# Ninety-five of 1024 softmax exponential tiles computed on VectorE instead of ScalarE, in a fused attention block on one core

## The chip, the cores and the metric

The kernel runs on one core of a Trainium2 chip. The metric is device time in microseconds for one execution of the whole program. A core has a matrix engine (TensorE, "PE" in the profile), a vector engine (VectorE, "DVE"), an activation engine (ScalarE, "ACT"), a general engine (GpSimd, "POOL") and a queue engine for transfers (SyncE, "SP"). Each works through its own instructions in order and waits on semaphores that the others raise. TensorE writes its results to PSUM, eight banks of 128 partitions by 512 fp32 values here; VectorE and ScalarE read them from there and write to SBUF.

## The reference

One block of multi-head self-attention in bf16, for a sequence of 2048, a width of 448 and 16 heads of 28:

```python
B, S, D = x.shape                 # 1, 2048, 448
H = 16
Dh = D // H                       # 28
qkv = (x @ wqkv).reshape(B, S, 3, H, Dh).transpose(2, 0, 3, 1, 4)
q, k, v = qkv[0], qkv[1], qkv[2]
scores = einsum("bhqd,bhkd->bhqk", q, k) * (Dh ** -0.5)
p = softmax(scores, axis=-1)
o = einsum("bhqk,bhkd->bhqd", p, v)
return o.transpose(0, 2, 1, 3).reshape(B, S, D) @ wo
```

## The kernel before

**Tiling.** The 16 heads form 4 groups of 4, and the 2048 queries form 4 chunks of 512. One group and one chunk make a unit; there are 16 units, group by group. In a unit the keys run over 16 blocks of 128. A tile is one head, one key block and one query chunk: 128 keys by 512 queries of scores. So a unit has 64 tiles, and the kernel 1024. The tiles are ordered by unit, then key block, then head.

**A tile's way.** TensorE forms the scores of a tile with one matmul (L579) over the 28 rows of the head's part of K and Q; the four heads of a group lie 32 partitions apart, so the matmuls of neighbouring tiles use different rows of the array. ScalarE takes the exponential of a group of tiles at once (L584: two tiles a group in unit 0, three after that), with the factor Dh^-0.5 as the activation's scale, and writes bf16 into one of 36 slots of `PT`. When the four tiles of a key block are done, four matmuls (L546, "PV") multiply them with V and add into the accumulator bank 7, one head in each quarter of the partitions. V carries a column of ones beside its 28, so the accumulator's row 28 of each head is the softmax denominator. No maximum is subtracted.

**A unit's end** (`post_unit`). VectorE copies the accumulator to SBUF (L501). TensorE gathers the denominators (L509), VectorE takes the reciprocals (L514), TensorE spreads them (L524), VectorE multiplies (L529). In the last four units, where all groups of a query chunk are complete, four output projections follow (L479), each evicted (L488, L490) and stored.

**Projections.** x is transposed on TensorE (L368) and projected to Q, K and V (L385, L402), and each result is evicted from PSUM (L354 on ScalarE for a few, L356 on VectorE for the rest). What unit 0 and 1 need is done early; 38 "late jobs" (14 Q, 12 K and 12 V pieces) have due times spread over the units.

**Banks.** Score groups alternate between banks 0 to 2 and 3 to 5 (0 to 1 and 2 to 3 in unit 0). Bank 7 is the accumulator. Bank 6, the pool "M", is the only one for late projections, both matmul steps of a unit's end, and the output projection. Early jobs use banks 4 to 6.

**What sets the order.** Every operation is added to a small planner (`_Prog`) with its engine, the operations it depends on, an assumed duration, and a priority that is a position in units: for a score group, its tile's position less 0.2. `schedule` walks through time with these assumed durations, and on each engine takes, among the operations that can start within 150 ns of the earliest, the one with the lowest priority number. An operation with `acq` takes a bank from a pool, and a `rel` gives it back. Assumed latencies are 120 ns between engines and 200 ns between dependent operations on one engine. The order that comes out is fixed in each engine's queue; on the chip only the semaphores act. Score groups are chained among themselves, exponentials among themselves, and PVs among themselves.

Of the kernel before, what the change touches and what calls it, by code (L numbers as in the profile page):

```python
# [6 lines left out]
AF = mybir.ActivationFunctionType  # L7
ALU = mybir.AluOpType
AX = mybir.AxisListType
FP32 = mybir.dt.float32  # L10
BF16 = mybir.dt.bfloat16
I32 = mybir.dt.int32

ENGINES = ("pe", "act", "dve", "pool", "sp")

# [213 lines left out]
RHI = 2.0 ** 40  # L229


def _fast(nc, x, wqkv, wo, out, n_heads=16):

    B, S, D = x.shape
    assert B == 1
    H = n_heads
    DH = D // H
    G = H // 4
# [7 lines left out]
    HC = H * 32  # L246
    GD = 4 * DH
    NPT = 36
    NOB = 4
    scale = float(DH) ** -0.5  # L250
    VONE = DH
    assert DH * H == D and G * 4 == H and DH + 1 <= 32 and NIT * IT == D and GD <= IT

    xf = x.rearrange("b s d -> (b s) d")
# [7 lines left out]
    with es:  # L262
        def sb(name, shape, dt):
            return es.enter_context(nc.sbuf_tensor(name, shape, dt))
# [6 lines left out]
        KT = sb("KT", [128, G, S], BF16)  # L271
        V = sb("V", [128, NK, HC], BF16)
        PT = sb("PT", [128, NPT * 512], BF16)
        OTS = sb("OTS", [128, 2, 512], FP32)
        RS = sb("RS", [128, NU * 16], FP32)
        OTN = sb("OTN", [128, G, S], BF16)
# [12 lines left out]
        def bank(b, n=1):  # L289
            return ps[:, b * 512:(b + n) * 512]  # L290
# [4 lines left out]
        def i32v(ap):  # L295
            return ap.bitcast(I32)

# [24 lines left out]
        ms_v0 = P.add("pool", lambda e: e.memset(V4[:, :, DH:32], 0.0), dur=1500, prio=-9, name="ms_v0")  # L322
        ms_v1 = P.add("pool", lambda e: e.memset(V4[:, :, VONE:VONE + 1], 1.0), deps=[ms_v0], dur=800, prio=-9, name="ms_v1")
        ms_wop = P.add("pool", lambda e: e.memset(i32v(wop.rearrange("p g d -> p (g d)")), 0), dur=900, prio=-8, name="ms_wop")
        ms_one = P.add("pool", lambda e: e.memset(ONE[:, :], 1.0), dur=100, prio=-7, name="ms_one")
        sel_op = P.add("dve", (lambda e: e.tensor_copy(SEL[:, :], id_f.rearrange("p (h r) -> p h r", r=32)[:, :, VONE])),
                       deps=[id_f_op], dur=100, prio=-6, name="sel")
# [11 lines left out]
        P.pool("M", [6])  # L339
        early_ev = []  # L340

        def job(name, prio, mm_ops, evac, early, evac_eng="dve", evac_dur=660, after=()):

            hold = []
            prev = None
            for k, (f, deps, dur) in enumerate(mm_ops):
                op = P.add("pe", (lambda e, f=f: f(e, hold[0].banks[0])),
                           deps=list(deps) + (list(early_ev) if (k == 0 and not early) else []), after=[prev] + list(after),
                           dur=dur, prio=prio, name=f"{name}_{k}", acq=(("E" if early else "M", 1) if k == 0 else None))
                if k == 0:  # L350
                    hold.append(op)
                prev = op
            if evac_eng == "act":
                fe = (lambda e: e.activation(evac[0](), evac[1](hold[0].banks[0]), AF.Identity))  # L354
            else:
                fe = (lambda e: e.tensor_copy(evac[0](), evac[1](hold[0].banks[0])))  # L356
            ev = P.add(evac_eng, fe, deps=[prev] + list(evac[2:]), dur=evac_dur, prio=prio, name=f"{name}_ev", rel=[(hold[0], 0)])
            if early:
                early_ev.append(ev)
            return ev  # L360
# [16 lines left out]
        def proj_qk(t, g, c, prio, early, eng="dve"):  # L377
            dst = KT if t == 1 else QT
            mms = []
            for it in range(NIT):  # L380
                def f(e, b, it=it):
                    ins = None
                    for h in range(4):
                        col = t * D + g * GD + h * DH
                        ins = e.matmul(ps[32 * h:32 * h + 32, b * 512:(b + 1) * 512], w_raw[0:IT, it, col:col + 32],  # L385
                                       xT[0:IT, it, c * 512:(c + 1) * 512], start=(it == 0), stop=(it == NIT - 1), tile_position=(0, 32 * h))
                    return ins
                mms.append((f, [xt_ev[(it, c)]] + ([dma_w[t]] if it == 0 else []), 300))
            kq_ev[(t, g, c)] = job(f"p{t}_{g}_{c}", prio, mms,
                                   ((lambda: dst[:, g, c * 512:(c + 1) * 512]), (lambda b: bank(b))), early, evac_eng=eng)  # L390

        v_ev = {}

# [28 lines left out]
        def late_jobs():  # L422
            todo = []
            for u, (g, c) in enumerate(units):
                if u < 2:
                    continue
                todo.append((u - 0.6, "q", g, c))
            for g in range(1, G):
                for c in range(NCH):
                    todo.append((g * NCH - 2.9 + 0.5 * c, "k", g, c))  # L430
                    todo.append((g * NCH - 2.7 + 0.5 * c, "v", g, c))
            for pr, kind, g, c in sorted(todo):
                if kind == "v":
                    proj_v(g, c, pr, False)
                else:
                    proj_qk(1 if kind == "k" else 0, g, c, pr, False)
        late_jobs()


        tiles = [(u, kt, h) for u in range(NU) for kt in range(NK) for h in range(4)]  # L440
        NT = len(tiles)
        groups = []
        n = 0
        k = 0
        while n < NT:
            if tiles[n][0] < LATE0:
                b0, w = (0, 2)[k % 2], 2
            else:
                b0, w = (0, 3)[k % 2], 3
            k += 1  # L450
            w = min(w, NT - n)
            groups.append((n, w, b0))
            n += w

        bank_last = {}
        pt_last = [None] * NPT
        pt_pos = 0
        tile_slot = {}
        tile_ev = {}
# [77 lines left out]
        def pv(u, kt):  # L537
            g, c = units[u]
            slots = [tile_slot[(u, kt, h)] for h in range(4)]

            def f_pv(e):
                ins = None
                for h in range(4):
                    hh = 4 * g + h
                    pi = slots[h]
                    ins = e.matmul(ps[32 * h:32 * h + 32, ACC * 512:(ACC + 1) * 512], V[:, kt, hh * 32:(hh + 1) * 32],  # L546
                                   PT[:, pi * 512:(pi + 1) * 512], start=(kt == 0), stop=(kt == NK - 1), tile_position=(0, 32 * h))
                return ins
            op = P.add("pe", f_pv, deps=list({id(tile_ev[(u, kt, h)]): tile_ev[(u, kt, h)] for h in range(4)}.values())
                       + [v_ev[(g, kt // 4)]] + ([acc_ev[0]] if kt == 0 else []),  # L550
                       after=[last_pv[0]], dur=300, prio=u + (kt + 3) / NK, name=f"PV{u}_{kt}")
            last_pv[0] = op
            for s in slots:
                pt_last[s] = op
            if kt == NK - 1:
                post_unit(u, op)

        last_pv = [None]
        pv_next = 0
        for gi, (n0, w, b0) in enumerate(groups):  # L560
            tl = tiles[n0:n0 + w]
            if pt_pos + w > NPT:
                pt_pos = 0
            p0 = pt_pos
            pt_pos += w
            deps = [bank_last.get(b0 + j) for j in range(w)]
            for (u, kt, h) in tl:
                g, c = units[u]
                deps += [kq_ev[(0, g, c)], kq_ev[(1, g, kt // 4)]]
            if tl[-1][0] >= LATE0:  # L570
                deps += early_ev
            u0, kt0, h0 = tl[0]
            pr = u0 + (kt0 + h0 / 4) / NK - 0.2

            def f_s(e, tl=tl, b0=b0):
                ins = None
                for j, (u, kt, h) in enumerate(tl):
                    g, c = units[u]
                    ins = e.matmul(bank(b0 + j), KT[32 * h:32 * h + DH, g, kt * 128:(kt + 1) * 128],  # L579
                                   QT[32 * h:32 * h + DH, g, c * QCH:(c + 1) * QCH], start=True, stop=True, tile_position=(32 * h, 0))  # L580
                return ins
            s = P.add("pe", f_s, deps=deps, after=[last_s[0]], dur=260, prio=pr, name=f"S{gi}")
            last_s[0] = s
            ex = P.add("act", (lambda e, p0=p0, w=w, b0=b0: e.activation(PT[:, p0 * 512:(p0 + w) * 512], bank(b0, w), AF.Exp, scale=scale)),  # L584
                       deps=[s] + [pt_last[p0 + j] for j in range(w)], after=[last_exp[0]], dur=100 + w * 427, prio=pr, name=f"E{gi}")
            last_exp[0] = ex
            for j, t in enumerate(tl):
                tile_slot[t] = p0 + j
                tile_ev[t] = ex
                bank_last[b0 + j] = ex  # L590
            while 4 * pv_next + 3 < n0 + w:
                u, kt, _ = tiles[4 * pv_next]
                pv(u, kt)
                pv_next += 1
# [734 lines left out]
```

## Time and profile before

| what | value |
|---|---|
| runs | 523.44, 524.41, 541.12 us, median 524.41 |
| profiled execution | 523.52 us, its span 521.7 us |
| mean granted TensorE clock | 0.685 of full |
| ScalarE busy | 467.2 us, of which the exponentials 463.1 us in 352 instructions |
| TensorE matmul busy | 420.0 us; scores 182.0, PV 135.3 |
| VectorE busy | 74.7 us in 130 instructions |
| ScalarE waiting for score matmuls | 25.2 us, 31 times |

The page gives busy time, which for instructions that overlap is less than the sum of their durations. A chain of waits follows the work back from the last instruction; a group's mean duration is that of one instruction, with the idle time of its engine just before it and what ended that.

### The profile page before, as it was taken

The numbers are of one execution on the slowest core, as the hardware profiler recorded it, in microseconds if no ns is written. First come the engines' busy times: TensorE is split into PE (matmuls) and PEld (weight loads), VectorE is DVE, ScalarE is ACT, GpSimd is POOL, SyncE is SP. The second block draws the span as 40 slices with busy tenths as digits, with TensorE's granted clock in tenths as the row PEclk, the third lists the DMA queues.
The fourth block names the chain that finished last, engine by engine and source line by source line (L and its number), as shares of the span: only waits on it lengthen the run. The fifth ranks groups of instructions, "written<-read, shape, count | busy, mean of one in ns | idle before, by whom it ended". The sixth has DMA issues, their size and how long they took to land.

```text
span 521.7 us, 7778 instructions
## 1 busy us (share of the span) xinstructions
PE 420.0 (80%) x3585; PEld 141.7 (27%) x3585; DVE 74.7 (14%) x130; ACT 467.2 (90%) x358; POOL 3.4 (1%) x9
## 2 busy tenths in 40 slices
PE   5998888898978788797978879787887968879763
PEld 2433333333323132131312213131221413214131
DVE  2433222322221000010100001010000200202020
ACT  2999999999998999989899998989989799898930
POOL 2000000000000000000000000000000000000000
PEclk9999999999895555555565555556555675857655
DMA  8000000000000000000000000000000000100001
GB/s 264 2 3 2 1 1 1 2 1 1 3 0 1 1 0 1 0 2 0 1 1 0 1 0 1 0 1 0 1 1 0 13 25 1 36 0 27 10 1 40
DMA packets 6518, 5.84 MB, mean 11 GB/s; under 512 B 592, under 2 KB 6480, under 8 KB 6480
## 3 DMA queue, kind: packets, MB, share of 16 engines
q1 hardware_dynamic: 5552, 4.48, 2.8%
q10 hardware_dynamic: 928, 0.80, 0.5%
q8 instruction: 30, 0.49, 0.4%
q14 instruction: 8, 0.07, 0.0%
HBM read 3.44 MB, written 1.84 MB: 10 GB/s over the span
## 4 chain that ended last, share of the span: by engine, by line
ACT 76%; PE 20%; DMA 1%; DVE 1%; issue 1%; ACTq 0%
ACT PT L584 75%; PE ps L579 5%; PE ps L524 5%; PE ps L509 4%; PE ps L479 3%; PE ps L546 2%; DMA w_raw<-in_wqkv_dram 1%; PE ps L385 1%; DVE OUTS L490 1%; DVE OTN L529 0%; ACT OUTS L488 0%; PE ps L402 0%; DVE OTS L501 0%; DVE KT L356 0%; ACTq L312 0%
## 5 line engine op out<-in xcount | busy, mean ns | idle before, releaser
L584 ACT ACTIVATE PT<-ps 128x1536 bf16<-128x1536 f32 (+1 forms) x352 | 463.1, 1544 | 25.6 <-PE ps L579 25.2
L579 PE MATMUL ps<-QT,KT 28*128 28x512 bf16 x1024 | 182.0, 517 | 83.0 <-ACT PT L584 81.7
L546 PE MATMUL ps<-PT,V 128*32 128x512 bf16 x1024 | 135.3, 523 | 0.9 <-ACT PT L584 0.9
L579 PEld LDWEIGHTS ps<-QT,KT 28*128 28x128 bf16 x1024 | 35.8, 96 | 228.5 <-ACT PT L584 216.5
L546 PEld LDWEIGHTS ps<-PT,V 128*32 128x32 bf16 x1024 | 27.2, 98 | 85.5 <-issue 83.0
L501 DVE COPY OTS<-ps 128x512 f32<-128x512 f32 x16 | 11.1, 692 | 262.4 <-PE ps L546 262.4
L385 PE MATMUL ps<-xT,w_raw 112*32 112x512 bf16 x512 | 41.5, 401 | 0.7 <-DMA w_raw<-in_wqkv_dram 0.2
L524 PE MATMUL ps<-id_f,RS 128*32 128x128 f32 x512 | 27.8, 387 | 0.4 <-DVE RS L514 0.4
L509 PE MATMUL ps<-SEL,OTS 128*128 128x4 f32 x128 | 26.6, 331 | 1.1 <-DVE OTS L501 0.8
L509 PEld LDWEIGHTS ps<-SEL,OTS 128*128 128x128 f32 x128 | 25.2, 293 | 8.2 <-DVE OTS L501 6.9
L524 PEld LDWEIGHTS ps<-id_f,RS 128*32 128x32 f32 x512 | 20.0, 154 | 7.3 <-issue 3.5
L479 PE MATMUL ps<-wop,OTN 128*128 128x448 bf16 x64 | 18.6, 424 | 3.3 <-DVE OUTS L490 1.4
L402 PE MATMUL ps<-w_raw,xT 112*128 112x112 bf16 x256 | 17.8, 214 | 0.3 <-DVE OTN L529 0.2
L385 PEld LDWEIGHTS ps<-xT,w_raw 112*32 112x32 bf16 x512 | 12.6, 98 | 14.4 <-issue 6.3
L529 DVE TENSOR_TENSOR OTN<-ps,OTS 128x512 bf16<-128x512 f32 x16 | 11.1, 692 | 35.0 <-PE ps L524 35.0
L356 DVE CAST KT<-ps 128x512 bf16<-128x512 f32 x16 | 11.1, 692 | 33.7 <-PE ps L385 33.7
L402 PEld LDWEIGHTS ps<-w_raw,xT 112*128 112x128 bf16 x256 | 13.1, 98 | 7.0 <-issue 5.7
L488 ACT ACTIVATE OUTS<-ps 128x448 bf16<-128x448 f32 x2 | 1.1, 544 | 14.7 <-PE ps L479 14.7
L356 DVE CAST QT<-ps 128x512 bf16<-128x512 f32 x15 | 10.4, 692 | 25.6 <-PE ps L385 25.6
L356 DVE CAST V<-ps 128x448 bf16<-128x448 f32 x16 | 10.0, 625 | 27.8 <-PE ps L402 27.8
L490 DVE CAST OUTS<-ps 128x448 bf16<-128x448 f32 x14 | 8.8, 625 | 19.9 <-PE ps L479 19.9
L368 PE MATMUL ps<-id_b,x_nat 128*112 128x128 bf16 x64 | 6.1, 248 | 5.7 <-DMA x_nat<-in_x_dram 5.7
(25 smaller groups left out, 31.4 us busy)
## 6 DMA issues: line engine op xcount, KB each, us to landing
x_nat<-in_x_dram SPq DMA_DIRECT2D x4, 448.0 KB, 7.4
out_dram<-OUTS SPq DMA_DIRECT2D x16, 112.0 KB, 1.7
w_raw<-in_wqkv_dram ACTq DMA_DIRECT2D x2, 392.0 KB, 6.4
w_raw<-in_wqkv_dram SPq DMA_DIRECT2D x1, 392.0 KB, 8.9
wop<-in_wo_dram SPq DMA_DIRECT2D x16, 24.5 KB
```

The lines of the kernel that those rows point to most:

```text
L356: fe = (lambda e: e.tensor_copy(evac[0](), evac[1](hold[0].banks[0])))
L385: ins = e.matmul(ps[32 * h:32 * h + 32, b * 512:(b + 1) * 512], w_raw[0:IT, it, col:col + 32], xT[0:IT, it, c * 512:(c + 1) * 512], start= ...
L402: ins = e.matmul(ps[:, b * 512 + j * GD:b * 512 + (j + 1) * GD], xT[0:IT, it, n * 128:(n + 1) * 128], w_raw[0:IT, it, 2 * D + g * GD:2 * D ...
L479: ins = e.matmul(bank(b)[:, 0:D], OTN[:, gg, n * 128:(n + 1) * 128], wop[:, gg, :], start=(gg == 0), stop=(gg == G - 1))
L490: fe = (lambda e: e.tensor_copy(OUTS[:, oi, :], bank(hold[0].banks[0])[:, 0:D]))
L501: accev = P.add("dve", (lambda e: e.tensor_copy(OTS[:, ub, :], bank(ACC))), deps=[last_pv, ots_last[ub]], dur=660, prio=pr, name=f"ACCEV{u}")
L509: ins = e.matmul(bank(b)[:, qt * 4:(qt + 1) * 4], OTS[:, ub, qt * 128:(qt + 1) * 128], SEL[:, :], start=True, stop=True)
L524: ins = e.matmul(ps[32 * h:32 * h + 32, b * 512 + qt * 128:b * 512 + (qt + 1) * 128], RS[:, i:i + 1].to_broadcast([128, 32]), id_f[:, :], ...
L529: nm = P.add("dve", (lambda e: e.tensor_tensor(OTN[:, g, c * QCH:(c + 1) * QCH], bank(n2.banks[0]), OTS[:, ub, :], ALU.mult)), deps=[n2], ...
L546: ins = e.matmul(ps[32 * h:32 * h + 32, ACC * 512:(ACC + 1) * 512], V[:, kt, hh * 32:(hh + 1) * 32], PT[:, pi * 512:(pi + 1) * 512], start ...
L579: ins = e.matmul(bank(b0 + j), KT[32 * h:32 * h + DH, g, kt * 128:(kt + 1) * 128], QT[32 * h:32 * h + DH, g, c * QCH:(c + 1) * QCH], start ...
L584: ex = P.add("act", (lambda e, p0=p0, w=w, b0=b0: e.activation(PT[:, p0 * 512:(p0 + w) * 512], bank(b0, w), AF.Exp, scale=scale)), deps=[s ...
```

## The change

95 of the 1024 tiles no longer go to ScalarE. A walk over the tiles with assumed costs (3.1 us a tile for VectorE, 0.464 for ScalarE, and a load for what VectorE does besides) picks them: one in unit 0, and 5 to 7 in each later unit, mostly 8 tiles apart, none among the last 12. The rest are grouped in threes as before, across the tiles picked out.

For a picked tile TensorE forms the scores in bank 6, with 29 rows in place of 28. Q's eviction multiplies by 65536 log2(e) Dh^-0.5, so that a score comes out as a fixed-point exponent with 16 fractional bits; the 29th row holds constants whose product adds the exponent's bias. That row is put there by a new matmul of one contraction row at the head of each Q and K projection. ScalarE's exponential gets the inverse scale.

VectorE then runs five operations. D1 limits the score to 0 and 255 in that format and converts it to int32. D2 takes the low 16 bits as the fraction f and forms w = ES f + EC. D3 and D4 form (w + EA) w and then (w + EB) w, a quartic in f. D5 adds that to the fixed-point number divided by 512 and writes int16, whose bits are read as bf16 by PV. There are 3 buffers for D1 and D2 to D4 (`DT`, `DW`) and 8 result slots (`PD`). A picked tile has its own score operation (SD), which isn't chained to the score groups, and a priority 14 tiles earlier than its position. PV's priority is one key block later than it was.

```diff
@@ job
             if evac_eng == "act":
-                fe = (lambda e: e.activation(evac[0](), evac[1](hold[0].banks[0]), AF.Identity))
+                fe = (lambda e: e.activation(evac[0](), evac[1](hold[0].banks[0]), AF.Identity, scale=1.0 if mul is None else mul))
+            elif mul is not None:
+                fe = (lambda e: e.tensor_scalar(evac[0](), evac[1](hold[0].banks[0]), mul, None, ALU.mult))
@@ proj_qk
+                    if it == 0:
+                        e.matmul(bank(b), CW[:, t, :], ONR[:, :], start=True, stop=False)
                     for h in range(4):
                         col = t * D + g * GD + h * DH
-                        ins = e.matmul(ps[32 * h:32 * h + 32, b * 512:(b + 1) * 512], w_raw[0:IT, it, col:col + 32],
-                                       xT[0:IT, it, c * 512:(c + 1) * 512], start=(it == 0), stop=(it == NIT - 1), tile_position=(0, 32 * h))
+                        ins = e.matmul(ps[32 * h:32 * h + DH, b * 512:(b + 1) * 512], w_raw[0:IT, it, col:col + DH],
+                                       xT[0:IT, it, c * 512:(c + 1) * 512], start=False, stop=(it == NIT - 1), tile_position=(0, 32 * h))
@@ selection
+        dve_load = [1.7 + (4 * 0.62 if u // NCH == G - 1 else 0.0) for u in range(NU)]
+        dve_load[0] += 22.0
+        for u_ in late_units:
+            dve_load[u_] += 0.69
+        DCOST, ACOST, LEAD = 3.1, 0.464, 1.0
+        t_a = t_d = 0.0
+        on_dve = set()
+        for i, (u, kt, h) in enumerate(tiles):
+            if i % 64 == 0:
+                t_d = max(t_d, t_a) + dve_load[u]
+            if t_d + DCOST <= t_a + LEAD and i < NT - 12:
+                t_d = max(t_d, t_a - 2.0) + DCOST
+                on_dve.add(i)
+            else:
+                t_a += ACOST
@@ pv
-                                   PT[:, pi * 512:(pi + 1) * 512], start=(kt == 0), stop=(kt == NK - 1), tile_position=(0, 32 * h))
+                                   p_ap, start=(kt == 0), stop=(kt == NK - 1), tile_position=(0, 32 * h))
...
-                       after=[last_pv[0]], dur=300, prio=u + (kt + 3) / NK, name=f"PV{u}_{kt}")
+                       after=[last_pv[0]], dur=300, prio=u + (kt + 4) / NK, name=f"PV{u}_{kt}")
@@ picked tiles
+                pr -= 14 / 64.0
+                di, pi = nd % NDB, nd % NPD
+                nd += 1
+                s = P.add("pe", (lambda e, tl=tl, hold=hold: s_mm(e, tl, [hold[0].banks[0]], DH + 1)), deps=deps,
+                          dur=220, prio=pr, name=f"SD{gi}", acq=("M", 1), slack=200.0)
+                hold.append(s)
+                T, W = DT[:, di, :], DW[:, di, :]
+                F16 = DT[:, di, :].bitcast(U16).rearrange("p (n two) -> p n two", two=2)[:, :, 0]
+                o1 = P.add("dve", (lambda e, T=T, s=s: e.tensor_scalar(T, bank(s.banks[0]), 0.0, 255.0 * 65536.0 - 1.0, ALU.max, ALU.min)),
+                           deps=[s, d_last[di]], dur=620, prio=pr, name=f"D1_{gi}", rel=[(s, 0)])
+                o2 = P.add("dve", (lambda e, F16=F16, W=W: e.tensor_scalar(W, F16, ES, EC, ALU.mult, ALU.add)),
+                           deps=[o1, d_last[di]], dur=610, prio=pr, name=f"D2_{gi}")
+                o3 = P.add("dve", (lambda e, W=W: e.scalar_tensor_tensor(W, W, EA, W, ALU.add, ALU.mult)),
+                           deps=[o2], dur=610, prio=pr, name=f"D3_{gi}")
+                o4 = P.add("dve", (lambda e, W=W: e.scalar_tensor_tensor(W, W, EB, W, ALU.add, ALU.mult)),
+                           deps=[o3], dur=610, prio=pr, name=f"D4_{gi}")
+                o5 = P.add("dve", (lambda e, W=W, T=T, pi=pi: e.scalar_tensor_tensor(PD[:, pi, :], T, 1.0 / 512.0, W, ALU.mult, ALU.add)),
+                           deps=[o4, slot_last.get(("D", pi))], dur=610, prio=pr, name=f"D5_{gi}")
+                d_last[di] = o5
+                tile_slot[tl[0]] = ("D", pi)
+                tile_ev[tl[0]] = o5
```

## The prediction

> **What bounds the kernel now.** I read the page first, for the share of each engine and the course of the clock.
>
> ```profile
> span 521.7 us, 7778 instructions
> ...
> PE 420.0 (80%) x3585; PEld 141.7 (27%) x3585; DVE 74.7 (14%) x130; ACT 467.2 (90%) x358; POOL 3.4 (1%) x9
> ...
> DVE  2433222322221000010100001010000200202020
> ACT  2999999999998999989899998989989799898930
> PEclk9999999999895555555565555556555675857655
> ```
>
> ScalarE is full from the second slice to the last but one, VectorE nearly empty from slice 13 on, and TensorE's granted clock falls to half at about 160 us. So I cut the span into stages (the table of stretches; columns: length, busy time of PE, weight loads, VectorE, ScalarE and POOL, clock, DMA).
>
> ```profile
> 12.90:42.60 29.70, 28.49 (x324) 11.69 (x324) 10.24 (x21) 29.54 (x32) 0.00 (x0) 1.00 0.01 2
> 42.60:161.10 118.50, 99.66 (x1260) 39.59 (x1260) 31.22 (x50) 117.14 (x88) 0.00 (x0) 0.96 0.01 2
> 191.50:345.20 153.70, 125.17 (x841) 35.95 (x841) 8.14 (x16) 144.95 (x108) 0.00 (x0) 0.51 0.00 1
> 345.20:500.05 154.85, 124.95 (x876) 39.02 (x876) 15.63 (x27) 142.97 (x105) 0.00 (x0) 0.61 0.03 10
> ```
>
> At full clock ScalarE is idle 1.4 us in 118.5. At half clock it is idle 8.8 in 153.7 and 11.9 in 154.9. The chain that ended last tells where (columns: start, length, work).
>
> ```profile
> 43.05 88.77 ACT PT L584 x66
> ...
> 167.14 24.29 ACT PT L584 x18
> 191.43 0.05 issue
> 191.48 0.61 PE ps L579 x3
> 192.09 1.87 PE ps L509 x8
> 193.96 0.55 PE ps L546 x3
> 194.51 0.54 PE ps L579 x3
> 195.05 1.86 PE ps L524 x32
> ```
>
> An exponential of three tiles costs 88.77 / 66 = 1.345 us of the path, or 24.29 / 18 = 1.349 at half clock: 0.450 us a tile. (Its own 1.58 us overlaps its neighbours.) At each unit's end the two normalisation steps, 1.87 us each at half clock, hold TensorE, and ScalarE starves about 2 us: its waits for score matmuls sum to 22.3 us between 161 and 500. Everything else is behind the exponentials, so taking tiles off ScalarE can pay.
>
> The prices come from the groups with shapes kept apart, and from VectorE's timeline.
>
> ```profile
> L584 ACT ACTIVATE PT<-ps 128x1536 bf16<-128x1536 f32 x320 | 433.5, 1583 | 24.0 <-PE ps L579 23.7
> L356 DVE CAST KT<-ps 128x512 bf16<-128x512 f32 x16 | 11.1, 692 | 33.7 <-PE ps L385 33.7
> L529 DVE TENSOR_TENSOR OTN<-ps,OTS 128x512 bf16<-128x512 f32 x16 | 11.1, 692 | 35.0 <-PE ps L524 35.0
> ```
>
> ```profile
> 13.27 1.09 DVE L356 COPY xT<-ps 112x512 bf16<-112x512 bf16 x3 [0.61 <-PE ps L368]
> ...
> 503.71 0.29 DVE L597 TENSOR_SCALAR CK<-RS 128x256 f32<-128x256 f32 x1
> 504.04 0.43 DVE L598 SCALAR_TENSOR_TENSOR CK<-RS,CK 128x256 f32<-128x256 f32 x1
> ```
>
> **Removed.** 95 tiles leave ScalarE: one in unit 0 (groups of two, 29.66 us for 64 tiles, 0.46 each) and 94 later: 0.46 + 94 x 0.450 = 42.8 us off the path, if nothing else becomes late.
>
> **Added on VectorE: five operations a tile.** D1 reads 512 fp32 from PSUM: 0.692, by the cast's row. D3, D4 and D5 take two inputs: 256 elements took 0.426 and the TENSOR_TENSOR at 512 took 0.692, so 0.692 each. D2 has one input in SBUF: by the 256-element TENSOR_SCALAR (0.294; same fixed 0.16, half the slope) 0.43, or 0.692 if the stepped 16-bit source loses that rate. Bodies: 3.20 to 3.46 us. A dependent operation starts 0.04 after the one before (504.00 to 504.04), so a chain alone takes 3.40 to 3.66. Independent operations overlap (three copies of 0.42 in 1.09, 0.085 saved on each), so two interleaved chains may take 2.77 to 3.03 a tile. Ends 2.77 and 3.66; there are three work buffers, so chains will partly interleave, and I take the middle, 3.25. Total 309 us beside the 74.7 already there: 384 us in a kernel of over 480, so VectorE is not the bound on average.
>
> In stretches it nearly is. Running the diff's selection rule by hand gives 5 to 7 tiles a unit after the first, and 79 of the 94 spacings are 8 tiles, thus 7 on ScalarE: 7 x 0.450 = 3.15 us. Each dense spacing lacks 3.25 - 3.15 = 0.10 us: 79 x 0.10 = 8 us. The ends are 0 and 79 x 0.51 = 40 us.
>
> What is queued behind: the score matmul of the next such tile (SD) needs bank 6, which D1 frees; TensorE takes its queue in order, so an SD early in its queue holds PV and the next scores, and then ScalarE. Normalisation, late projections and output projection share that bank, and the unit's eviction stands in VectorE's queue among the D operations. Eight result slots let tiles be made far ahead of their PV, which covers single delays.
>
> **Added on TensorE.** An SD stands alone where three scores stand side by side: one packet of three took 0.32 us until the next start at full clock and 0.54 at half, and one alone costs no less than 512 columns of that. 95 x 0.32 to 0.54 is 30 to 51 us, less 31 packets saved (10 to 17). At half clock a unit needs (19.3 + 6.3) x 0.54 + 16 x 0.55 + 3.74 = 26.4 us of TensorE, against 24.1 now; ScalarE needs 58 x 0.45 = 26.1. It fits in about 28, with 1.6 us to spare. I cost it at nothing; if the spare goes, the first rival holds.
>
> **Added to the projections**: one matmul of one row ahead of each of 32 Q and K jobs, 0.3 us each. The two at the start lie on the path and four run in unit 0, where TensorE is 28.49 of 29.70 busy: 0 to 1.8 us, I take 1.5. The 26 later ones sit beside exponentials. Four small memsets run before the first x lands (5.7 us), under that load. The Q scaling replaces a copy of the same size: nothing.
>
> **The clock.** In the trace TensorE goes to half speed after 150 us although its longest wait for ScalarE there (the weight loads of L579) is 1.2 us, and is back at full speed for 4 us only after some 6 us without a gap (162 to 168). The Trainium skill, "TensorE: Matmul & The Clock Gate", section "Why this matters for your kernels", asks for idle gaps over about 3 us before the clock falls. This trace disagrees, with its 1.2 us; by the page the half clock and its unit-end waits would be absent and the sum about 470. The trace decides.
>
> A rule that speaks against the change stands in "VectorE: DVE Perf Modes", section "The DRAIN you can't avoid": the next operation cannot issue until the pipe is empty, so five operations always cost five whole ones. By it the sum would be near the first rival's end, 522; the three overlapping copies (1.09 us, not 1.26) say it is not so strict.
>
> **Sum.** The profiled execution took 523.5 us (span 521.7), close to the median of 524.4. 523.5 - 42.8 + 1.5 + 8 = 490.2, rounded to 490. The tail after the last exponential (500 us on) is untouched, since the last 12 tiles stay on ScalarE.
>
> **Rivals.**
> 1. VectorE paces, or TensorE at half clock does. For: dense spacings of 3.15 us against up to 3.66; 1.6 us of TensorE spare. Against: the gaps of 16 to 24 tiles and eight slots. With the full 40 us lost: 523.5 - 42.8 + 1.5 + 40 = 522; its middle 512.
> 2. Slower: an SD reaches the head of TensorE's queue while bank 6 waits behind two queued VectorE operations (2 x 0.69 = 1.38 us). A score packet now waits 0.36 us on average for ScalarE in the half-clock stage (63.6 us over 179 waits between 161 and 500), so that much lateness is covered. It loses from the point where each of 95 waits exceeds 0.45 + 0.36 = 0.81; at 1.38 the time is 523.5 + 95 x 0.57 = 578. For: one bank for all of it, and an order fixed beforehand from assumed durations (0.61 an operation) that are shorter than the rows. Against: VectorE is free a fifth of the time.
> 3. More TensorE work closes its gaps, the clock stays up, and the 22.3 us of unit-end waits mostly vanish (19.8 of them fall between 160 and 470): 490 - 19.8 = 470. For: 168 to 172 us. Against: 1.7 busy of 2 us did not lift it.
> 4. The change does not do what it says, because VectorE's PSUM reads slow the exponentials: at 10%, 929 x 0.045 = 42 us, no gain, 524. Against: 1.345 us a group with VectorE a quarter busy, 1.349 with it idle.
>
> **How the numbers follow.** Forecast 0.45 (own range 482 to 503); rival 1 0.17 (503 to 523); rival 2 0.19 (523 to 580); rival 3 0.14 (465 to 482); rival 4 0.05. The measurement can tell about 2%, so faster means under 514: 0.45 + 0.14 + 0.10 of rival 1 = 0.69. Within: 0.07 + 0.03 of rival 2 + 0.04 of rival 4 = 0.14. Slower than 535: 0.16 + 0.01 = 0.17. The range 476 to 535 leaves out some 0.06 of rival 3 below and 0.14 of rival 2 above.
>
> **What would show it.** Groups of three stay at 1.35 us and number about 289. VectorE's busy time is near 384 us; D2's row at 0.43 or 0.69 settles it. ScalarE's waits for score matmuls are near 35 us; over 60, traced to TensorE waiting for D1's line, is rival 2. A granted clock well over 0.685 is rival 3. The prediction is wrong if a tile takes over 3.6 us on VectorE, if SDs wait for bank 6 at length, or if unit ends hold ScalarE longer than 2 us.

## The result, and the profile after

The changed kernel takes 539.76 us (median of 4 runs, 537.47 to 541.39), the kernel before beside it 524.41 (523.44 to 527.49, and one run of 541.12). Some runs of one and the same kernel take some per cent longer than its others, so runs more than 1.5% above a kernel's fastest are given but not compared, here and below. The ratio is 1.0276, with a 95% interval of 1.0206 to 1.0345: slower, by some 15 us, where the forecast was 34 us faster. The profiled execution took 539.61 us, its span is 537.7.

The page of the changed kernel, by its first lines, the course of ScalarE and of the clock, and the chain that ended last by engine:

```profile
span 537.7 us, 8275 instructions
...
PE 478.3 (89%) x3617; PEld 156.7 (29%) x3617; DVE 346.0 (64%) x609; ACT 432.7 (80%) x327; POOL 3.4 (1%) x9
...
ACT  2897777777988888897898899778798979798940
PEclk9995555555555655795657597555656576595855
...
PE 54%; ACT 33%; DVE 10%; DMA 1%; issue 1%; ACTq 0%
```

ScalarE is no longer full, and the first half clock stands in the fourth slice, where before it stood in the thirteenth. TensorE now makes up 54% of the chain. The same stretches as in the prediction (length, busy time of PE, weight loads, VectorE, ScalarE, POOL, clock, DMA):

```profile
12.90:42.60 29.70, 28.02 (x302) 11.70 (x301) 15.11 (x30) 27.81 (x31) 0.00 (x0) 0.98 0.03 5
42.60:161.10 118.50, 111.64 (x784) 35.21 (x784) 77.84 (x136) 92.06 (x67) 0.00 (x0) 0.50 0.00 1
191.50:345.20 153.70, 138.95 (x1137) 46.68 (x1135) 111.99 (x193) 133.71 (x99) 0.00 (x0) 0.66 0.00 1
345.20:500.05 154.85, 141.32 (x1007) 44.00 (x1005) 110.74 (x195) 132.23 (x96) 0.00 (x0) 0.60 0.02 7
```

The second row carries the result. Before, the clock there was 0.96 and ScalarE worked 117.14 of 118.50 us; now the clock is 0.50 throughout, TensorE is busy 111.64 us and ScalarE works 92.06. That is 25 us of ScalarE's time lost in one stretch. The prices of VectorE's part are in the groups with shapes kept apart (busy, mean ns of one, idle time before, its releaser):

```profile
L649 ACT ACTIVATE PT<-ps 128x1536 bf16<-128x1536 f32 x288 | 398.5, 1481 | 72.9 <-PE ps L637 71.0
...
L665 DVE TENSOR_SCALAR DT<-ps 128x512 int32<-128x512 f32 x95 | 65.5, 689 | 34.0 <-PE ps L637 33.6
L671 DVE SCALAR_TENSOR_TENSOR DW<-DW 128x512 f32<-128x512 f32 x95 | 65.2, 686 | 0.8
L673 DVE SCALAR_TENSOR_TENSOR PD<-DT,DW 128x512 int16<-128x512 int32 x95 | 64.8, 682 | 0.1
L669 DVE SCALAR_TENSOR_TENSOR DW<-DW 128x512 f32<-128x512 f32 x95 | 64.5, 679 | 0.8
...
L667 DVE TENSOR_SCALAR DW<-DT 128x512 f32<-128x512 uint16 x95 | 40.2, 423 | 1.4
```

D1, D3, D4 and D5 cost 0.68 to 0.69 us, D2 0.42. The waits (in total, times, longest) tell who is late:

```profile
ACT PT L649 <- PE ps L637: 73.7, 85, 2.7
...
PEld ps L637 <- DVE DT L665: 20.1, 37, 1.3
...
PEld ps L413 <- DVE DT L665: 11.0, 18, 1.3
...
PE ps L637 <- DVE DT L665: 5.2, 14, 0.8
```

ScalarE waits 73.7 us for scores, against 25.2 before. So the account closes on ScalarE: its exponentials' busy time fell from 463.1 to 428.5 us (34.6 less), its waits for scores rose by 48.5, and the first exponential starts 1.4 us later (14.3 against 12.9). That is 15.3 us more, and the span grew by 16.0. The page's row for all exponentials:

```profile
L649 ACT ACTIVATE PT<-ps 128x1536 bf16<-128x1536 f32 (+1 forms) x321 | 428.5, 1440 | 75.6 <-PE ps L637 73.7
```

TensorE waits for D1 in small pieces on several lines: 41.1 us by its weight loads and 9.7 us by its matmuls, never over 1.3 us at a time. D1 (L665) holds 4% of the chain, some 21 us.

Two things in TensorE's records are new. First, the projections have moved. Each row below gives the matmuls' shortest, median and longest duration (ns) and their first and last start (us); first the kernel before, then the changed one.

```profile
L385 PE MATMUL ps<-xT,w_raw x512: 377/381/634, 7.6 to 150.9; 112*32 112x512 bf16 x171
```

```profile
L416 PE MATMUL ps<-xT,w_raw x512: 379/605/634, 8.3 to 471.6; 112*28 112x512 bf16 x171
```

They ended at 151 us, at full clock; now the last starts at 471.6 and the median duration is that of half clock. In the order of TensorE's queue the last projection stood behind score tile 307 before, and stands behind tile 932 now. The planner did that: a picked tile's score matmul (SD) has a priority 14 tiles ahead of its position, needs no other bank than 6, and so takes it from the late projections, whose numbers are higher. Second, the clock drops at 42 us; before, it dipped from 134.5 to 138 us and fell for longer at 155. All engines by single microseconds, first the kernel before, then the changed one (same columns):

```profile
39.00:40.00 1.00, 1.00 (x12) 0.25 (x12) 0.06 (x1) 1.00 (x2) 0.00 (x0) 1.00 0.07 16
40.00:41.00 1.00, 0.47 (x4) 0.09 (x2) 0.63 (x1) 1.00 (x2) 0.00 (x0) 1.00 0.00 0
41.00:42.00 1.00, 1.00 (x18) 0.67 (x17) 0.00 (x0) 1.00 (x2) 0.00 (x0) 1.00 0.00 0
42.00:43.00 1.00, 0.78 (x15) 0.34 (x11) 0.57 (x1) 0.56 (x1) 0.00 (x0) 1.00 0.00 0
```

```profile
39.00:40.00 1.00, 0.80 (x9) 0.20 (x7) 1.00 (x2) 1.00 (x2) 0.00 (x0) 1.00 0.00 0
40.00:41.00 1.00, 0.47 (x5) 0.09 (x2) 1.00 (x3) 1.00 (x2) 0.00 (x0) 1.00 0.06 16
41.00:42.00 1.00, 0.80 (x8) 0.20 (x6) 1.00 (x3) 1.00 (x2) 0.00 (x0) 0.80 0.00 0
42.00:43.00 1.00, 0.69 (x3) 0.10 (x1) 1.00 (x3) 1.00 (x2) 0.00 (x0) 0.50 0.00 0
43.00:44.00 1.00, 1.00 (x9) 0.25 (x10) 1.00 (x2) 0.91 (x2) 0.00 (x0) 0.50 0.00 0
```

Before, projections ran among the scores there. With them pushed back TensorE had less to do from 39 to 43 us, and waited for ScalarE, which was full. The clock fell, and but for 3.4 us (181.5 to 185) it stayed at half until 222 us, although TensorE was busy 169.0 of the 179 us from 43 to 222. That the thin stretch made it fall is read from the order in time; no experiment changes that stretch alone.

### The profile page after: what moved, and what is told of

It is laid out like the page before. It is cut to its first block, busy times and chain, and to the rows that moved or that the text cites. A ratio compares the mean times of both kernels' runs of the same rounds, so it can differ in the third digit from the quotient of the medians.

```text
span 537.7 us, 8275 instructions
## 1 busy us (share of the span) xinstructions
PE 478.3 (89%) x3617; PEld 156.7 (29%) x3617; DVE 346.0 (64%) x609; ACT 432.7 (80%) x327; POOL 3.4 (1%) x9
## 4 chain that ended last, share of the span: by engine, by line
PE 54%; ACT 33%; DVE 10%; DMA 1%; issue 1%; ACTq 0%
ACT PT L649 33%; PE ps L637 17%; PE ps L603 11%; PE ps L416 8%; PE ps L580 5%; PE ps L565 5%; DVE DT L665 4%; PE ps L433 3%; PE ps L535 3%; PE ps L413 2%; DVE DW L669 1%; DMA w_raw<-in_wqkv_dram 1%; DVE DW L671 1%; DVE PD L673 1%; DVE OTS L557 1%; DVE DW L667 1%
## 5 line engine op out<-in xcount | busy, mean ns | idle before, releaser
L649 ACT ACTIVATE PT<-ps 128x1536 bf16<-128x1536 f32 (+1 forms) x321 | 428.5, 1440 | 75.6 <-PE ps L637 73.7
L637 PE MATMUL ps<-QT,KT 28*128 28x512 bf16 (+1 forms) x1024 | 200.2, 540 | 35.1 <-ACT PT L649 27.7
L637 PEld LDWEIGHTS ps<-QT,KT 28*128 28x128 bf16 (+1 forms) x1024 | 37.5, 97 | 181.0 <-ACT PT L649 107.3
L665 DVE TENSOR_SCALAR DT<-ps 128x512 int32<-128x512 f32 x95 | 65.5, 689 | 34.0 <-PE ps L637 33.6
L671 DVE SCALAR_TENSOR_TENSOR DW<-DW 128x512 f32<-128x512 f32 x95 | 65.2, 686 | 0.8
L669 DVE SCALAR_TENSOR_TENSOR DW<-DW 128x512 f32<-128x512 f32 x95 | 64.5, 679 | 0.8
L673 DVE SCALAR_TENSOR_TENSOR PD<-DT,DW 128x512 int16<-128x512 int32 x95 | 64.8, 682 | 0.1
L416 PE MATMUL ps<-xT,w_raw 112*28 112x512 bf16 x512 | 57.0, 543 | 0.0
L603 PE MATMUL ps<-PD,V 128*32 128x512 bf16 x95 | 52.3, 551 | 0.0
L667 DVE TENSOR_SCALAR DW<-DT 128x512 f32<-128x512 uint16 x95 | 40.2, 423 | 1.4
L433 PE MATMUL ps<-w_raw,xT 112*128 112x112 bf16 x256 | 23.5, 256 | 1.4 <-DVE DT L665 1.4
L535 PE MATMUL ps<-wop,OTN 128*128 128x448 bf16 x64 | 19.4, 439 | 3.4 <-DVE OUTS L546 1.4
```

The costliest lines, as they stand in the source:

```text
L416: ins = e.matmul(ps[32 * h:32 * h + DH, b * 512:(b + 1) * 512], w_raw[0:IT, it, col:col + DH], xT[0:IT, it, c * 512:(c + 1) * 512], start= ...
L433: ins = e.matmul(ps[:, b * 512 + j * GD:b * 512 + (j + 1) * GD], xT[0:IT, it, n * 128:(n + 1) * 128], w_raw[0:IT, it, 2 * D + g * GD:2 * D ...
L637: ins = e.matmul(bank(b), KT[32 * h:32 * h + rows, g, kt * 128:(kt + 1) * 128], QT[32 * h:32 * h + rows, g, c * QCH:(c + 1) * QCH], start= ...
L665: o1 = P.add("dve", (lambda e, T=T, s=s: e.tensor_scalar(T, bank(s.banks[0]), 0.0, 255.0 * 65536.0 - 1.0, ALU.max, ALU.min)), deps=[s, d_l ...
L667: o2 = P.add("dve", (lambda e, F16=F16, W=W: e.tensor_scalar(W, F16, ES, EC, ALU.mult, ALU.add)), deps=[o1, d_last[di]], dur=610, prio=pr, ...
L669: o3 = P.add("dve", (lambda e, W=W: e.scalar_tensor_tensor(W, W, EA, W, ALU.add, ALU.mult)), deps=[o2], dur=610, prio=pr, name=f"D3_{gi}")
```

## The experiments

These theories stood at the start or came up on the way. **A**: picked score matmuls displace the projections into the time of half clock, and TensorE at half clock becomes the bound. **B** (the prediction's second rival): TensorE waits on bank 6 for VectorE. **C**: the changed projections cost by themselves. **K**, formed after the fifth run: the one-row matmul occupies TensorE but counts for little in what keeps its clock up; **L** is its rival, that it costs only its own time. **D**: only the picked tiles of units 0 to 4 hurt.

**The projections' part alone.** No tile is picked; Q's scale, row 28 and the one-row matmuls stay.

```diff
-            if t_d + DCOST <= t_a + LEAD and i < NT - 12:
+            if False and i < NT - 12:
```

> Only the projection part of the change (row of constants by a matmul of one contraction row, Q scaling, 28 columns in place of 32, PV one key block later); no tile goes to VectorE. Theory A (TensorE sets the time of the changed kernel: its clock is at half from 42 us on and the late projections moved into that time): 520 to 532 us, the clock falls near 150 us as before, since nothing competes with the late projections for bank 6. Theory B (waits for bank 6 behind VectorE's chains): the same 520 to 532. Theory C (the extra matmul in each Q and K projection is the loss): 535 us or more.

Measured: 524.7 us (median of the 8 compared of 12 runs), ratio 1.0008 (0.9978 to 1.0038). With the projections early in TensorE's queue (the last behind score tile 313) this part costs nothing in the runs compared, and C falls as stated. The other four runs took 544.2 to 588.2 us; why is not shown.

**A short chain on VectorE.** D2, D3 and D4 work on 8 of 512 elements, the buffers being set once.

```diff
+        ms_dw = P.add("dve", lambda e: e.memset(DW[:, :, :], 0.0), dur=1600, prio=-10.5, name="ms_dw")
...
-                o3 = P.add("dve", (lambda e, W=W: e.scalar_tensor_tensor(W, W, EA, W, ALU.add, ALU.mult)),
+                o3 = P.add("dve", (lambda e, W=W: e.scalar_tensor_tensor(W[:, 0:8], W[:, 0:8], EA, W[:, 0:8], ALU.add, ALU.mult)),
```

> The changed kernel with D2, D3 and D4 run over 8 of 512 elements (the quartic is left out for the rest; work left out on purpose), so that a tile costs VectorE about 1.7 us instead of 3.2, with the same planned order. Theory A: 528 to 545 us, since TensorE's work and clock stay. Theory B: 515 us or less, since D1 and with it bank 6 comes free up to 1.5 us earlier for each of 95 tiles.

Measured: one run of 521.3 us at a mean clock of 0.670; the other three took 529.2 to 536.0 at 0.631 to 0.646, and there is no interval. VectorE's busy time fell from 346 to 228 us, a third. The compared run lies between A's range and B's, and the three others fall in A's. So B is not excluded, and its share stays open.

**Late projections first.** Their priority number is lower by 8 units, so that they come first; picks begin with unit 5 (74 tiles), and each SD depends on the last projection.

```diff
+                pr -= 8.0
...
-            if t_d + DCOST <= t_a + LEAD and i < NT - 12:
+            if u >= 5 and t_d + DCOST <= t_a + LEAD and i < NT - 12:
...
+            if kind == "D":
+                deps += late_ev
```

> All 38 late projections get priority over the rest, and the tiles for VectorE are picked only from unit 5 on, their score matmuls after the last late projection (74 tiles). Theory A: full clock until about 130 to 150 us, and 490 to 508 us: 524 less 74 x 0.45 = 33 us, plus up to 17 for the half clock later. Theory B: the loss per tile stays, (540 - 481) / 95 x 74 = 46 us on top of 524 - 33, so 525 to 540 us.

Measured: 506.7 us, ratio 0.9638 (0.959 to 0.9686). The clock from 42.6 to 161.1 us is 0.91. A's numbers are met, but three things were changed at once.

**Score matmuls twice**, in packets of ScalarE's tiles only: 929 more matmuls.

```diff
-                for (u, kt, h), b in zip(tl, banks):
+                for (u, kt, h), b in list(zip(tl, banks)) * (2 if rows == DH else 1):
```

> The changed kernel with every score packet for ScalarE issued twice into the same banks, so that TensorE's gaps are filled. Theory A, where a denser queue holds the full clock: granted clock above 0.9 and 515 us or less, although TensorE does some 100 us more work at full clock. Theory A, where density does not lift the clock: about 310 x 0.54 = 167 us more TensorE work at half clock, 650 to 700 us. Theory B: the waits for VectorE are untouched, 535 to 570 us.

Measured: 547.0 and 547.9 us at a mean clock of 0.77 (two more runs took 565.9 and 566.2 at 0.725), no interval. Neither of A's cases came: the mean clock rose from 0.624 to 0.77, and so 929 matmuls more cost only some 8 us. B's range holds the time, but B says nothing of the clock. The added matmuls brought the clock up.

**The bias added in D1.** The one-row matmul and row 28 go; D1 adds the bias, and its upper limit goes.

```diff
-                        e.matmul(bank(b), CW[:, t, :], ONR[:, :], start=True, stop=False)
...
-                o1 = P.add("dve", (lambda e, T=T, s=s: e.tensor_scalar(T, bank(s.banks[0]), 0.0, 255.0 * 65536.0 - 1.0, ALU.max, ALU.min)),
+                o1 = P.add("dve", (lambda e, T=T, s=s: e.tensor_scalar(T, bank(s.banks[0]), 127.0 * 65536.0, 0.0, ALU.add, ALU.max)),
```

> The changed kernel with the exponent bias added by D1 (add, then max with 0; the upper limit of the score is left out), so that the extra matmul in each of 32 Q and K projections, the row of constants and its memsets are gone. The projections stand as late in the order as in the changed kernel (the last after 929 score tiles). Theory A (TensorE at half clock bounds, and the projections moved into that time): 17 us less TensorE work, 520 to 533 us. Theory B (waits for bank 6 behind VectorE): 535 to 542.

Measured: 500.3 and 506.5 us (two more runs took 517.4 and 517.6), ratio 0.96 (0.9528 to 0.9672). By their mean of 503.4 that is 36 us less, more than the 16.9 us that the 32 matmuls were busy, although the projections still end late (the last behind tile 929). It lies below the ranges of A and B alike, so theory K was formed.

**The bias in D1 and SDs after the last projection**: the edit before, with picks from unit 5 on and the dependency of the third experiment, the projections at their own due times.

> Tiles for VectorE only from unit 5 on (74), their score matmuls not before the last late projection, late projections with their own due times (the last after 307 score tiles, as before the change), and the bias in D1. Theory A: 495 to 504 us. Theory B: 520 us or more. A version that may beat both kernels.

Measured: 493.4 us (492.9 to 493.8), ratio 0.9409 (0.939 to 0.9429). It is the fastest of all, and beats both kernels. It lies just under A's range, and B's is missed.

**Picks from unit 5 on, projections late**, with the one-row matmul and without the dependency:

> The same pick of tiles from unit 5 on, but their score matmuls may run before the late projections, which compete with them for bank 6 and are pushed back (the last after 900 score tiles). Nothing else differs from the next kernel. Theory A: 518 to 532 us, since about half of the projections fall in half-clock time. Theory D (what hurt was only the picked tiles in units 0 to 4): the same as the next kernel within 4 us.

Measured: 531.8 us (528.8 to 532.4, and one run of 536.9), ratio 1.0113 (1.0071 to 1.0155), at the upper end of A's range; the last projection stands behind tile 900.

**The same with the dependency**, so that the projections come first:

> The pick from unit 5 on with the score matmuls of picked tiles after the last late projection (after 313 score tiles); constants by the extra matmul as in the change. Theory A: 498 to 507 us. Theory D: the same as the kernel before it within 4 us.

Measured: 494.1 and 498.1 us, with mean clocks of 0.707 and 0.710; two more runs took 516.2 and 556.0, with 0.671 and 0.587. By the two compared the order is worth some 36 us, and D falls. Two runs give no interval, so the price is taken from a second pair below.

**Constants on 64 rows.** The extra matmul uses 64 rows in place of one; its constants are divided by 64. Its count and place are those of the changed kernel.

```diff
-        CW = sb("CW", [1, 2, 128], BF16)
-        ONR = sb("ONR", [1, 512], BF16)
+        CW = sb("CW", [64, 2, 128], BF16)
+        ONR = sb("ONR", [64, 512], BF16)
...
-        ms_cq = P.add("dve", lambda e: e.memset(CW4[:, 0, :, CROW], QCONST), deps=[ms_c0], dur=100, prio=-11, name="ms_cq")
+        ms_cq = P.add("dve", lambda e: e.memset(CW4[:, 0, :, CROW], QCONST / 64.0), deps=[ms_c0], dur=100, prio=-11, name="ms_cq")
```

> The changed kernel with the extra matmul of each Q and K projection over 64 contraction rows in place of one, each row holding a 64th of the constant, so that its result and its length stay. Theory K (a matmul with one row at work counts as idleness for TensorE's clock): the clock rises from 0.624 to 0.65 or more and the time falls to 525 us or less. Theory L (the extra matmul costs its time on a bounding TensorE and its place in the queue, whatever its rows): 536 to 543 us.

Measured: 516.3 us (510.1 to 517.4), ratio 0.9809 (0.9726 to 0.9893), mean clock 0.69 against 0.624. With the same work in the same order, 23 us (539.8 - 516.3) hang on the rows of 32 matmuls: K's numbers are met and L falls. The two traces agree, to 0.1 us, until the first of these matmuls after the clock's fall. First the changed kernel, TensorE's timeline (start, length, work):

```profile
53.49 1.05 PE L603 MATMUL ps<-PT,V 128*32 128x512 bf16 x8
54.47 0.60 PE L413 MATMUL ps<-ONR,CW 1*128 1x512 bf16 x1
55.01 0.61 PE L416 MATMUL ps<-xT,w_raw 112*28 112x512 bf16 x4
```

Then the kernel with 64 rows:

```profile
53.55 1.05 PE L603 MATMUL ps<-PT,V 128*32 128x512 bf16 x8
54.53 0.61 PE L413 MATMUL ps<-ONR,CW 64*128 64x512 bf16 x1
55.06 0.40 PE L416 MATMUL ps<-xT,w_raw 112*28 112x512 bf16 x4
```

Both matmuls take the same 0.6 us, in a TensorE without a gap since 48.5 us. Behind the one with 64 rows the next packet takes 0.40 us: the clock is back. Behind the one-row matmul it takes 0.61. The windows from there on, first the changed kernel, then the one with 64 rows:

```profile
54.00:56.00 2.00, 2.00 (x16) 0.31 (x8) 0.38 (x1) 1.06 (x1) 0.00 (x0) 0.50 0.00 0
56.00:58.00 2.00, 2.00 (x18) 0.39 (x15) 0.39 (x1) 1.45 (x1) 0.00 (x0) 0.50 0.02 4
58.00:60.00 2.00, 2.00 (x15) 0.35 (x12) 1.04 (x3) 1.80 (x2) 0.00 (x0) 0.50 0.00 0
60.00:62.00 2.00, 2.00 (x21) 1.30 (x18) 1.76 (x3) 1.11 (x2) 0.00 (x0) 0.50 0.03 8
62.00:64.00 2.00, 2.00 (x16) 0.52 (x14) 1.22 (x2) 1.88 (x2) 0.00 (x0) 0.50 0.00 0
```

```profile
54.00:56.00 2.00, 2.00 (x24) 0.47 (x20) 0.43 (x1) 1.28 (x2) 0.00 (x0) 0.73 0.00 0
56.00:58.00 2.00, 1.85 (x27) 0.46 (x19) 0.92 (x2) 2.00 (x2) 0.00 (x0) 1.00 0.01 4
```

So the one-row matmul does not pull the clock down here (it fell at 42 us in both); where it runs, the clock does not come back. That it alone holds the clock down is not shown: from 55.0 to 65.5 us the changed kernel's TensorE works without a gap and without such a matmul, and the clock stays at 0.50. Over the stretch up to 161 us ScalarE works 102.18 us instead of 92.06:

```profile
42.60:161.10 118.50, 107.12 (x864) 35.60 (x864) 88.91 (x156) 102.18 (x76) 0.00 (x0) 0.64 0.00 1
```

**64 rows, 63 of them with zero weights**, the moving rows all ones:

```diff
-        ms_cq = P.add("dve", lambda e: e.memset(CW4[:, 0, :, CROW], QCONST), deps=[ms_c0], dur=100, prio=-11, name="ms_cq")
+        ms_cq = P.add("dve", lambda e: e.memset(CW4[0:1, 0, :, CROW], QCONST), deps=[ms_c0], dur=100, prio=-11, name="ms_cq")
```

> The changed kernel with the extra matmul over 64 contraction rows of which 63 hold zeros as weights (the moving rows are all ones). If the clock goes by the rows that an instruction uses: like 64 rows of constants, 508 to 520 us, clock near 0.69. If it goes by the data that change in the array: like one row, 535 to 542 us, clock near 0.625.

Measured: 517.3 us, ratio 0.9895 (0.9842 to 0.9948), clock 0.694 in the profiled execution. In this kernel the rows that the instruction uses count, not whether the added weights are zero.

**64 rows, picks from unit 5 on, projections first**:

> Tiles from unit 5 on after the last late projection, with the extra matmul over 64 rows. With one row that kernel's runs lay between 494 and 556 us with the granted clock between 0.71 and 0.59. Theory K: all runs within 490 to 500 us. Theory L: the spread stays, some runs above 510.

Measured: 495.6 us (494.3 to 496.7), ratio 0.9441 (0.9413 to 0.9469), within K's range. But 494.1 and 498.1 us with one row lie beside it: in this order the rows make no difference to the runs compared. Why two of the four one-row runs took over 510 us is not shown. The stretch up to 161 us and, from the waits, ScalarE's:

```profile
42.60:161.10 118.50, 108.58 (x1291) 41.20 (x1289) 34.34 (x55) 116.14 (x88) 0.00 (x0) 0.99 0.01 2
```

```profile
ACT PT L652 <- PE ps L640: 29.7, 30, 2.7
```

ScalarE's time in that stretch and its waits over the whole span are nearly those of the kernel before (117.14 and 25.2).

**64 rows, the same picks, projections late.** It differs from the one before only by the SDs' dependency, so it prices the order alone, with no one-row matmul in either:

> Tiles from unit 5 on, late projections pushed back behind their score matmuls (the last after 900 score tiles), with the extra matmul over 64 rows. The kernel with the projections first and 64 rows took 495.6 us. If the place of the projections costs by itself: 508 to 520 us. If all of the loss was the matmul of one row: within 4 us of 495.6.

Measured: 531.0 us (529.2 to 532.9, and one run of 543.8), ratio 1.0147 (1.0112 to 1.0181): 35 us more than with the projections first, and above the 508 to 520 that was expected. With one row it was 531.8, so here too the rows make no difference. ScalarE's row and its waits:

```profile
42.60:161.10 118.50, 104.48 (x879) 31.44 (x877) 47.37 (x79) 106.94 (x80) 0.00 (x0) 0.67 0.00 1
```

```profile
ACT PT L650 <- PE ps L638: 56.9, 67, 3.1
```

VectorE's timeline of this kernel shows how far an SD made ahead can block the bank (idle time before, and what ended it, in brackets):

```profile
131.55 0.69 DVE L385 CAST KT<-ps 128x512 bf16<-128x512 f32 x1 [1.90 <-PE ps L416]
145.81 0.69 DVE L558 COPY OTS<-ps 128x512 f32<-128x512 f32 x1 [13.56 <-PE ps L604]
175.36 0.69 DVE L558 COPY OTS<-ps 128x512 f32<-128x512 f32 x1 [28.86 <-PE ps L604]
179.38 0.69 DVE L674 SCALAR_TENSOR_TENSOR PD<-DT,DW 128x512 int16<-128x512 int32 x1 [3.33 <-PE ps L604]
180.11 0.69 DVE L666 TENSOR_SCALAR DT<-ps 128x512 int32<-128x512 f32 x1
```

An SD ran on TensorE in a packet at 132.52 us; the next D1 runs at 180.11, behind two accumulator copies and a D5 whose result slot PV had not yet freed. For some 47 us bank 6 was held by scores that nobody could use. TensorE ran no projection between 131.5 and 192.7 us. The normalisation of the unit whose accumulator was copied at 145.81 began at 180.86, that of the next (175.36) at 186.54. So the 35 us hold both the projections' late place and this blocked bank; no run separates them.

**Fewer picked tiles**, with the bias in D1 and the projections first (`DCOST` 5.0). The pick gives 32 tiles in place of 74, not the 30 that the expectation counts with:

> The fastest version so far (bias in D1, tiles from unit 5 on after the last late projection) with 30 tiles on VectorE in place of 74 (an assumed cost of 5.0 in the pick). If ScalarE sets the time in the half-clock stage, 44 x 0.45 = 20 us more, 513 us. If TensorE at half clock sets it there, about the same or less: 490 to 500, since 44 single score matmuls go (24 us) and 15 packets come back (8 us).

Measured: 512.8 us, ratio 0.9799 (0.9734 to 0.9864). Against the kernel with 74 tiles (493.4) that is 19.4 us for 42 tiles, 0.46 us each.

## Why the prediction was wrong, point by point

**What bounds the kernel: right for the kernel before, and no longer true of the one after.** The tile's worth of 0.450 us measures 0.46 where ScalarE still sets the end. The 42.8 us as a whole show as 34.6 of busy time, which fits that a group that had to wait no longer overlaps its neighbour (85 waits in place of 31).

**VectorE's chain: right.** Bodies add up to 300.2 us over 95 tiles, 3.16 each, just under the 3.20 of the estimate. VectorE's busy time was 346.0 us, not 384: less 75 us for its other work, 2.86 us a tile, near the lower end of 2.77 and not the middle of 3.25, so the chains interleave well. D5 waited 0.1 us in all, and no PV waited long for it. The rule quoted from the Trainium skill ("VectorE: DVE Perf Modes", section "The DRAIN you can't avoid") was read too strictly: the same section lets a next operation that is not held start earlier, and this trace agrees, with 2.86 us of busy time a tile against the 3.16 of five whole operations. The 8 us for dense spacing are bounded by the kernel with the bias in D1 and the projections first: 74 tiles at 0.450 from the 524.2 us beside it give 490.9, and it took 493.4. If each of the 74 was worth that much, some 2.5 us are left for it there.

**"The 26 later ones sit beside exponentials": wrong, and worth 23 us.** The matmuls of one row were costed at nothing, as work beside other work. Their own time matters little while the projections come early, as the kernel without picked tiles shows. But 64 rows in their place, with all else equal, took 23 us off the changed kernel. The working asked how long these instructions are and not what they do to the clock, which it took over from the trace of before.

**TensorE's added work, "I cost it at nothing; if the spare goes, the first rival holds": wrong.** The balance of a unit at half clock (26.4 us of TensorE against 26.1 of ScalarE) held no projection, since in the trace of before they were all over by 151 us. The working named the bank that SDs share with the late projections, and asked what waits behind an SD on TensorE; it didn't ask who gets the bank when both are ready. With the projections moved behind the clock's fall, Q's and K's took 57.0 us instead of 41.5, those of V 23.5 instead of 17.8, and the long fall itself came 113 us earlier, where TensorE lacked the filling that the projections had been. In the pick from unit 5 on, the order alone is worth 35 us, the blocked bank 6 included.

**The two failures together** are what was missed. From 539.8, 64 rows lead to 516.3. Projections first lead from there to 495.6, with 21 tiles fewer, which at 0.46 are 9.7 us; so it would be some 486 us at equal tiles (an estimate, if each of the 21 kept its worth). The forecast of 490 lies beside that. The two prices don't simply add: with picks from unit 5 on, the rows changed nothing in either order (494.1 and 498.1 against 495.6, and 531.8 against 531.0), while the order was worth some 35 us with either number of rows. So the order, which put the projections late, is the larger failure, and the 23 us of the rows belong to the changed kernel's own pick.

**The rivals.** The first had the engine right in its second half ("TensorE at half clock does"), but its bound of 522 us came from VectorE's chain alone; the time went 18 us past it. The second had the right side and the wrong place: its sign, more than 60 us of waits on ScalarE, was there (73.7), but TensorE's waits for D1's line are 41.1 us by weight loads and 9.7 by matmuls, none over 1.3 us, and its full price of 1.38 us for each of 95 tiles did not come. D1's 4% of the chain stays with it, and the run with a third less work on VectorE does not settle its share. Bank 6 did decide: who was served first was worth 35 us in the pick from unit 5 on. The third saw that the clock would move, and not which way. The fourth is refuted: in the fastest kernel a group of three still costs the path 25.64 / 19 = 1.349 us in a stretch in which VectorE was busy for 23.61 of 25.64 us. The row of its chain:

```profile
278.30 25.64 ACT PT L645 x19
```

**What stays open.** The step from 516.3 to 495.6 took the SDs out of units 0 to 4 along with the moved projections, so the waits for bank 6 in those units are not told apart from the projections' place there. Nor is it known why the clock stayed at half from 55.0 to 65.5 us in the changed kernel. A bank of its own for the SDs wasn't tried: all eight are in use. From how many rows on an instruction counts, what exactly is counted, and why the rows mattered in one pick and not in the other, is not settled.

## What to carry to other kernels

When work is added to a shared bank under a fixed order, ask who is now served first, and follow the work that loses its place to the stage where it lands; its price there can be another one. Read the clock as a result of the change, not as a given: work that fills TensorE can be worth more than its busy time says. An experiment that moves only the order, and one that changes only an instruction's shape, separated here what the busy times could not.

## What the runs showed of the hardware

A matmul of one contraction row takes as long as one of 64 (0.60 and 0.61 us at half clock), but a kernel with 32 of them had a mean clock of 0.624, against 0.69 with 64 rows, even where 63 of these held zero weights (0.694). A TensorE without a gap was not enough to raise the clock: in the changed kernel it stayed at 0.50 from 55.0 to 65.5 us with TensorE busy all the time and no one-row matmul among its work. And 929 more score matmuls raised the mean clock to 0.77, so that added work on the bound engine cost only some 8 us.

The Trainium skill, "TensorE: Matmul & The Clock Gate", section "Part 1: The HAM clock gate (the "warmup" mystery)", has the clock follow how busy TensorE was in a free-running window of about 3.4 us. The fall at 42 us, some 3 us after the thin stretch began, fits that length. The 10.5 us at half clock without a gap do not fit it: by busy time alone the clock should have come back. That the rows an instruction uses can weigh in it is what these runs add.
